# The first stage of a chunked-attention and mixture-of-experts kernel in another order, and its score products in 64x64 tiles of TensorE

## The chip, the cores and the metric

The kernel runs on one core of a Trainium2 chip, in one launch. The metric is device time in microseconds (us) of one execution. The engines are TensorE (PE in the profile, with PEld for its weight loads), VectorE (DVE), ScalarE (ACT), GpSimd (POOL) and SyncE (SP), which here only issues transfers. The kernel before takes 537.81 us (median of 3 runs, 537.52 to 538.01).

## The reference, cut to what matters

Three stages follow each other on 4 x 768 = 3072 tokens.

```
# 1. chunked linear attention, per batch and head (8 heads, head_dim 32, state 16)
cum = cumsum(log a) in a chunk;  L = exp(cum_i - cum_j) for i >= j
y   = ((C B^T) * L) x  +  exp(cum) * (C state)
state = decay * state + (B * decay_from_j)^T x
# 2. gated MLP on [3072, 256], d_ff 1536
y = (silu(x @ w_gate) * (x @ w_val)) @ w_out
# 3. routed MLP: 8 experts, one expert for each token, 256 -> 1024 -> 256, gated by its probability
```

The inputs are float32 (the MLP's weights are float64 and come as pairs of 32-bit words). The output is float32, [3072, 256].

## The kernel before, in words

The sequence is cut into 24 units of 128 tokens of one batch, numbered u, six for each batch. Four units make a block of 512 tokens; there are six blocks. For each unit four things happen in the first of the reference's stages:

- `weigh(u)` (L274) multiplies x by the decays W, on VectorE or GpSimd, into `xw`.
- `scores_mm(u)` (L282) makes on TensorE the state products (L292, into `pc`, 64 columns) and the score products (L298, B C^T, 256 columns, same buffers). Both use tiles of the array of 64 rows and 32 columns, eight of which work side by side. Each product is one of float32 and appears in the trace as two passes, so L298 has 16 passes in a unit.
- `scores_m(u)` (L302) masks the scores on VectorE (`mt`), and `states(u)` (L309) carries the state on (`st`, `sv`, `se`).
- `values_mm(u)` (L332) makes the outputs (L344, L354, also in 64x32 tiles); `values_out(u)` and `values_low(u)` scale them on VectorE and split them into a high and a low part (`xt`, L375 and L381).

Around it, `decode(f, parts)` (L397) turns one twelfth of the MLP's weights (768 KB, loaded by `load_w`) from float64 words into a high and a low float32 part: part 0 on ScalarE, parts a, b and c on VectorE (L409, L412, L416), part 2 on ScalarE (`wh`, L419), part 3 (`wl`, L421). `mlp1_mm` (L430) and `mlp1_down` (L459) are the MLP's products, in 128x128 weights and 512 columns, three for each product of float32.

The order of all work is written out by hand: each engine executes its instructions in the order in which the program issues them, and waits come from the data and from buffers used in turn (three PSUM buffers "a" for `pc` and `py`, three "g", four for x and for C). SyncE's queue carries nearly all loads, in order.

`first_block` (L807) holds the stage that the change reorders. It loads, makes the decays of the first block (`setup_ln`, `setup_decay`, `setup_cum`), and then walks units 0 to 3: in each turn it issues the scores of unit u+1 and the values of unit u, then `keep_busy(n)`, which multiplies a constant by itself n times into a PSUM buffer that nobody reads, then the VectorE work. Decodes of the first weights stand between. After the fourth turn the MLP of block 0 begins (24 turns i, with units 4 to 11 in between), then `block(b)` for blocks 2 to 5, and at last the routed stage. `emit_d` and `emit_u` spread the decays of one block over heads (GpSimd, then TensorE and ScalarE); block 1's are wanted from unit 4 on.

Of the kernel before, what the change touches and what calls it, by code (L numbers as in the profile page):

```python
# [9 lines left out]
F32 = mybir.dt.float32  # L10
# [19 lines left out]
NBLK = T // BLK  # L30
# [90 lines left out]
def kernel(  # L121
# [5 lines left out]
    nc = tc.nc  # L127
# [34 lines left out]
    def load(u):  # L162
        if u >= NU or u in raw:
            return
        r = {}
        xbb = ap_.tile([128, 512], F32, name="xbb", tag="xbb", bufs=4)
        nc.sync.dma_start(out=xbb, in_=I["xbb"][:, u])
        r["x"] = xbb[:, 0:DM].rearrange("k (h d) -> k h d", h=8)
        r["b"] = xbb[:, DM:DM + 128]
        r["bt"] = xbb[:, DM + 128:]  # L170
        r["c"] = ap_.tile([128, 2, 4, 64], F32, name="cbd", tag="cbd", bufs=4)
        nc.sync.dma_start(out=r["c"].rearrange("p r h i -> p (r h i)"), in_=I["cbd"][:, u])
        raw[u] = r

    def setup_loads():
        nc.sync.dma_start(out=at[:, 0:2], in_=I["at"][:, 0:2])
        nc.scalar.dma_start(out=c1[:, 0:C_R16], in_=I["cst"][:, 0:C_R16])
        nc.scalar.dma_start(out=c1[:, C_R16:C1], in_=I["cst"][:, C_R16:C1])
        nc.scalar.preload_act_table_set("natural_log_exp_and_others")

    def setup_ln(b0, b1):
        a = at[:, b0:b1]
        nc.vector.tensor_scalar(out=a, in0=a, scalar1=1e-6, scalar2=1.0, op0=ALU.max, op1=ALU.min)
        nc.scalar.activation(out=a, in_=a, func=AF.Ln)

    def setup_decay(b0, b1):
        p = ps_g("pw", (128, b1 - b0, 32))
        nc.tensor.matmul(out=p, lhsT=c1[:, C_S:C_S + 128], rhs=at[:, b0:b1, 0:32], start=True, stop=True)
        nc.scalar.activation(out=W[:, b0:b1], in_=p, func=AF.Exp)
# [11 lines left out]
    def keep_busy(n):  # L201

        if not idle_t:
            idle_t.append(ps.tile([128, 2, 256], F32, tag="y0", bufs=1, name="pi"))
        for _ in range(n):
            nc.tensor.matmul(out=idle_t[0], lhsT=r32[:, 0],  # L206
                             rhs=r32.rearrange("p g j -> p (g j)").unsqueeze(1).to_broadcast([128, 2, 256]),
                             start=True, stop=True)

    def silu_first():  # L210
# [32 lines left out]
    def cum_store(b0, n, p):  # L243
        nc.vector.tensor_copy(out=eb[:, 8 * b0:8 * b0 + 8 * n], in_=p)
# [37 lines left out]
    def scores_mm(u):  # L282


        r = raw[u]
        r["pc"] = [ps_a([128, 512], "pc") for _ in range(2)]
        r["pS"] = [p[:, 256:320] for p in r["pc"]]
        for q in range(4):
            for i in range(2):
                if i == 0 or u % NC != NC - 1:  # L290
                    k = slice(64 * i, 64 * i + 64)
                    nc.tensor.matmul(out=r["pS"][i][32 * q:32 * q + 32], lhsT=r["b"][k, 32 * q:32 * q + 32],  # L292
                                     rhs=r["xw"][k, 2 * q:2 * q + 2], start=True, stop=True,
                                     tile_position=(64 * i, 32 * q))
        for q in range(4):
            for g in range(2):
                k = slice(64 * g, 64 * g + 64)
                nc.tensor.matmul(out=r["pc"][g][32 * q:32 * q + 32, 0:256], lhsT=r["bt"][k, 32 * q:32 * q + 32],  # L298
                                 rhs=r["c"][k, q // 2].rearrange("p h i -> p (h i)"), start=True, stop=True,
                                 tile_position=(64 * g, 32 * q))  # L300

    def scores_m(u):  # L302
        r = raw[u]
# [84 lines left out]
    def load_w(f, e=nc.sync):  # L388
        if f >= NF:
            return  # L390
        wr[f] = keep.tile([128, 768, 2], I32, name="wraw", tag="raw", bufs=3)
        e.dma_start(out=wr[f], in_=I["mw"][f].bitcast(I32).rearrange("p (n t) -> p n t", t=2))
# [414 lines left out]
    def first_block():  # L807

        setup_loads()
        load(0)  # L810
        nc.sync.dma_start(out=at[:, 2:], in_=I["at"][:, 2:])
        load_w(0)
        load(1)
        load(2)
        load_w(1)
        load(3)
        load_w(2)
        setup_ln(0, 2)
        setup_decay(0, 2)
        setup_cum(0, 1)  # L820
        weigh(0, nc.vector)
        scores_mm(0)
        cum_split(0, 1)
        setup_ones()
        setup_ln(2, NBLK)
        setup_decay(2, NBLK)
        scores_m(0)
        emit_u(0, emit_d(0))
        cum_store(0, 1, cum_ends(0, 1, cum_ends_d(0, 1)))
        states(0)  # L830
        cum_pairs(1, 8)
        weigh(1, nc.gpsimd)
        weigh(2, nc.gpsimd)
        keep_busy(1)
        decode(0, 0, "a", "b")
        for u in range(4):
            scores_mm(u + 1)
            values_mm(u)
            keep_busy((5, 7, 6, 7)[u])
            scores_m(u + 1)  # L840
            states(u + 1)
            values_out(u)
            if u == 0:
                decode(0, "c")
            if u == 1:
                decode(1, "a")
            if u == 2:
                decode(1, "b")
            values_low(u)
            load(u + 4)  # L850
            if u == 0:
                load_w(3)
                nc.sync.dma_start(out=c2, in_=I["cst"][:, C1:C_END])
                weigh(3, nc.gpsimd)
                decode(0, 2)
                decode(0, 3, low=nc.gpsimd)
            if u == 1:
                setup_cum(1, 2)
                decode(1, 0)
                d = emit_d(1)  # L860
                weigh(4, nc.gpsimd)
            if u == 2:
                silu_first()
                emit_u(1, d)
                weigh(5, nc.gpsimd)
        decode(1, "c", 2, 3)
        decode(2, 0)
        load_w(4)

        todo = {0: 2, 1: 3, 2: 4, 4: 5, 6: 6, 8: 7, 10: 8, 12: 9, 14: 10, 15: 11}  # L870
        units = {0: 4, 1: 5, 3: 6, 5: 7, 13: 8, 16: 9, 19: 10, 22: 11}
        for i in range(2 * NF):
            q, f = divmod(i, HALF)
            b, f = q % 2, f + HALF * (q // 2)
            u = units.get(i)
            w = todo.get(i, NF)
            if i + 1 in units and units[i + 1] > 4:
                weigh(units[i + 1] + 1, nc.vector if i < 16 else nc.gpsimd)
            if u == 7:
                scores_mm(u + 1)  # L880
                values_mm(u)
                values_out(u)
                values_low(u)
            p = mlp1_mm(b, 0, BLK, f)
            if u is not None and u != 7:
                scores_mm(u + 1)
                values_mm(u)
            if len(late) == LAG:
                mlp1_down(*late.pop(0))
            late.append((b, 0, BLK, f))  # L890
            decode(w, 1)
            h = mlp1_h(p, BLK)
            if w < NF:
                load_w(w + 3)
                decode(w + 1, 0)
            decode(w, 2)
            if u is not None and u != 7:
                values_out(u)
            decode(w, 3)
            if i in (20, 21):  # L900
                turn_y(0, 2 * i - 40)
                turn_y(0, 2 * i - 39)
            if i == 23:
                route_b(0)
            mlp1_split(h, b, 0, BLK, f)
            if i in (7, 13):
                take_part(0 if i == 7 else 1)
            if i == 19:
                take_y(0)
            if u is not None:  # L910
                if u != 7:
                    values_low(u)
                    scores_m(u + 1)
                    states(u + 1)
                load(u + 4)
            if i == 6:
                scores_m(8)
                cum_split(1, 2)
            if i == 7:
                dd.append(cum_ends_d(1, 2))  # L920
            if i == 8:
                cum_store(1, 2, cum_ends(1, 2, dd.pop()))
                cum_pairs(8, NU)
                states(8)
            if i == 9:
                dd.append(emit_d(2))
            if i == 10:
                emit_u(2, dd.pop())
            if 16 <= i < 20:
                setup_route(i - 16)  # L930
            if i == 22:
                route_a(0)
            if i == 21:
                dd.append(emit_d(3))
            if i == 23:
                emit_u(3, dd.pop())
# [190 lines left out]
```

## Time and profile before

| | before |
|---|---|
| time, median of 3 runs | 537.81 us (537.52 to 538.01) |
| time of the profiled execution | 539.36 us |
| its span | 537.6 us |
| PE busy | 510.0 us (95%), 4592 matmuls |
| DVE busy | 297.2 us (55%) |
| ACT busy | 211.5 us (39%) |
| POOL busy | 105.9 us (20%) |
| mean granted clock of TensorE | 0.984 |

The span is what the trace covers; the time of the same execution is 1.8 us longer. Shares of busy time are averages over stages: the stretches that the change touches are seen in the rows below. In a timeline row the two numbers in front are the start and the time covered, "xN" is the count of instructions merged, and brackets show how long the engine sat idle before it and what ended that.

### The profile page before, as it was taken

The page shows a single profiled execution, that of the slowest core. Times are in us where ns is not written, and L with a number is a line of the kernel's source. Part 1 is how long each engine was busy: PE and PEld are TensorE (multiplying, and loading weights), DVE is VectorE, ACT ScalarE, POOL GpSimd, SP SyncE. Part 2 cuts the span into 40 slices and gives each one's busy share as a digit, 9 for nine tenths or more (in the row PEclk, how much of TensorE's full clock was granted, in tenths as well). Part 3 has the DMA queues.
Part 4 walks back from the last instruction along what each step waited for, and adds up shares of the span by engine and source line. Part 5 has one row for each costly group of instructions (what it writes and reads, how often), then busy time and mean ns, then how long its engine had stood idle before and what let it go on. Part 6 is the DMA issues. An engine that isn't in the chain of part 4 may idle for free.

```text
span 537.6 us, 11261 instructions
## 1 busy us (share of the span) xinstructions
PE 510.0 (95%) x4592; PEld 420.9 (78%) x4592; DVE 297.2 (55%) x643; ACT 211.5 (39%) x391; POOL 105.9 (20%) x127
## 2 busy tenths in 40 slices
PE   5889899999999999999999999999999999999990
PEld 3667688778878878887778778888889989999880
DVE  5788787785454454446443555365376664646320
ACT  3454356443333333333333333344454354535220
POOL 2300000131040050003200033403036425250210
PEclk9899899999999999999999999999999999999996
DMA  8755232111023122103100102434097534431100
GB/s 291 291 178 195 101 103 93 41 51 40 22 77 28 56 63 40 40 21 100 21 2 2 41 2 62 176 104 53 2 138 165 173 118 137 143 116 41 39 21 21
DMA packets 20838, 45.84 MB, mean 85 GB/s; under 512 B 4656, under 2 KB 8496, under 8 KB 20784
## 3 DMA queue, kind: packets, MB, share of 16 engines
q1 hardware_dynamic: 17424, 38.39, 24.9%
q0 software_dynamic: 3072, 6.41, 3.8%
q8 instruction: 37, 0.61, 0.6%
q10 hardware_dynamic: 288, 0.30, 0.2%
q14 instruction: 17, 0.14, 0.1%
HBM read 38.59 MB, written 6.50 MB: 84 GB/s over the span
## 4 chain that ended last, share of the span: by engine, by line
PE 80%; issue 9%; DVE 5%; POOL 2%; DMA 1%; ACT 1%; SPq 0%; POOLq 0%; DVEq 0%
PE py L469 19%; PE pg L441 18%; PE pv L441 17%; PE ph L758 8%; PE po L779 8%; PE pt L553 2%; PE pc L298 2%; POOL out L793 1%; PE py L354 1%; PE py L344 1%; PE pi L206 1%; PE pc L292 1%; PE px L747 1%; DMA xbb<-in_xbb 1%; DVE wv L412 1%
## 5 line engine op out<-in xcount | busy, mean ns | idle before, releaser
L441 PE MATMUL pg<-xt,wh 128*128 128x512 f32 x288 | 93.6, 406 | 1.9 <-ACT wh L419 1.8
L441 PE MATMUL pv<-xt,wh 128*128 128x512 f32 x288 | 91.0, 397 | 0.6 <-DVE h L449 0.6
L449 DVE TENSOR_TENSOR h<-h,pv 128x512 f32<-128x512 f32 x72 | 49.4, 686 | 66.5 <-PE pv L441 58.0
L456 DVE TENSOR_TENSOR hl<-h,hh 128x512 fp32r<-128x512 f32 x72 | 50.3, 698 | 61.7 <-ACT hh L455 61.4
L758 PE MATMUL ph<-xt,hl 128*128 128x512 f32 x288 | 72.7, 394 | 0.0
L779 PE MATMUL po<-hl,hh 128*128 128x256 f32 x384 | 70.1, 283 | 0.0
L441 PEld LDWEIGHTS pv<-xt,wh 128*128 128x128 f32 x288 | 54.4, 190 | 14.1 <-DVE h L449 1.4
L441 PEld LDWEIGHTS pg<-xt,wh 128*128 128x128 f32 x288 | 52.5, 190 | 13.2 <-ACT wh L419 2.0
L779 PEld LDWEIGHTS po<-hl,hh 128*128 128x128 f32 x384 | 60.3, 188 | 2.1
L455 ACT CAST hh<-h 128x512 fp32r<-128x512 f32 x72 | 44.6, 620 | 41.2 <-DVE h L449 41.2
L448 ACT ACTIVATE h<-pg 128x512 f32<-128x512 f32 x72 | 42.7, 593 | 42.1 <-PE pg L441 42.1
L614 POOL DMA_INDIRECT slots<-ids,si x24 | 26.0, 1083 | 168.3 <-DVE si L606 163.5
L758 PEld LDWEIGHTS ph<-xt,hl 128*128 128x128 f32 x288 | 51.7, 188 | 9.2
L469 PE MATMUL py<-hh,wh 128*128 128x512 f32 x144 | 58.6, 407 | 0.0
L441 PE MATMUL pg<-xt,wl 128*128 128x512 f32 x144 | 57.5, 399 | 0.2 <-DVE wl L421 0.2
L441 PE MATMUL pv<-xt,wl 128*128 128x512 f32 x144 | 56.9, 395 | 0.0
L469 PE MATMUL py<-hl,wh 128*128 128x512 f32 x144 | 56.8, 395 | 0.0
L469 PE MATMUL py<-hh,wl 128*128 128x512 f32 x144 | 56.8, 395 | 0.0
L779 PE MATMUL po<-hl,hl 128*128 128x256 f32 x192 | 53.9, 281 | 0.2 <-DVE hl L767 0.2
L767 DVE SCALAR_TENSOR_TENSOR hl<-ph,hh 128x512 fp32r<-128x512 f32 x48 | 33.0, 688 | 32.9 <-ACT hh L766 32.8
L766 ACT ACTIVATE hh<-ph 128x512 fp32r<-128x512 f32 x48 | 28.8, 600 | 42.9 <-PE ph L758 27.6
L779 PEld LDWEIGHTS po<-hl,hl 128*128 128x128 f32 x192 | 36.1, 188 | 0.4 <-DVE hl L767 0.4
(140 smaller groups left out, 675.1 us busy)
## 6 DMA issues: line engine op xcount, KB each, us to landing
eraw<-in_ew SPq DMA_DIRECT2D x24, 512.0 KB, 3.8
wraw<-in_mw SPq DMA_DIRECT2D x12, 768.0 KB, 4.3
xbb<-in_xbb SPq DMA_DIRECT2D x24, 256.0 KB, 4.5
cbd<-in_cbd SPq DMA_DIRECT2D x24, 256.0 KB, 4.4
yd<-yr SPq DMA_DIRECT2D x6, 528.0 KB, 3.2
slots<-ids,si POOLq DMA_INDIRECT x24, 8.1
xg<-yd,idx POOLq DMA_INDIRECT x24, 4.9
out<-ob,idx POOLq DMA_INDIRECT x24, 2.5
```

What stands on the lines that cost most here:

```text
L298: nc.tensor.matmul(out=r["pc"][g][32 * q:32 * q + 32, 0:256], lhsT=r["bt"][k, 32 * q:32 * q + 32], rhs=r["c"][k, q // 2].rearrange("p h i ...
L441: nc.tensor.matmul(out=t, lhsT=w[:, f, o:o + 128], rhs=xt[:, xp, k, cs], start=n == 0, stop=n == 5)
L448: nc.scalar.activation(out=h, in_=p[0], func=AF.Silu)
L449: nc.vector.tensor_tensor(out=h, in0=h, in1=p[1], op=ALU.mult)
L455: nc.scalar.copy(out=hh, in_=h)
L456: e.tensor_tensor(out=hl, in0=h, in1=hh.bitcast(F32), op=ALU.subtract)
L469: nc.tensor.matmul(out=yb[b][d][:, c:c + m], lhsT=w[:, f, o:o + 128], rhs=h, start=first and n == 0, stop=last and n == 2, skip_group_chec ...
L614: i = nc.gpsimd.indirect_dma_start(out=slots[0:E * upto], out_offset=bass.IndirectOffsetOnAxis(ap=si[:, s:s + 1], axis=0), in_=ids[g][:, o ...
L758: nc.tensor.matmul(out=p, lhsT=self.hl[:, w, o:o + 128], rhs=self.xt[:, xp, k], start=n == 0, stop=n == 5)
L766: nc.scalar.activation(out=hh, in_=p, func=AF.Relu)
L767: nc.vector.scalar_tensor_tensor(out=hl, in0=p, scalar=0.0, in1=hh.bitcast(F32), op0=ALU.max, op1=ALU.subtract)
L779: nc.tensor.matmul(out=self.po[s // 2][:, s % 2], lhsT=h[:, q], rhs=self.hl[:, w, o:o + DM], start=f == 0 and n == 0 and s % 2 == 0, stop= ...
```

## The change

- `setup_loads`: the load of the table of ScalarE's functions is issued ahead of the second constants' transfer rather than behind it.
- SyncE's order: unit 1's x and C come right behind unit 0's, ahead of the other blocks' `at` and the first weights; the third weights (`load_w(2)`) come behind unit 4's loads rather than before the loop.
- The logarithms and decays of blocks 1 to 5 (`setup_ln(2, NBLK)`, `setup_decay(2, NBLK)`) and the cumulated decays for blocks 2 to 5 (`setup_cum(1, 2)`) are issued later or, for the last, one turn earlier: in the first turn of the loop. `emit_d(1)` and `emit_u(1)` move up from turns 1 and 2 to before the loop and turn 0.
- `weigh(1)` is issued on GpSimd ahead of the states of unit 0.
- Weight 0's parts a, b, c are decoded together in turn 0 (before: a and b ahead of the loop, c in turn 0).
- Constant products: 0, 2, 2 and 1 in turns 0 to 3 in place of 5, 7, 6 and 7, none ahead of the loop in place of 1, and each on float32 rather than float32r operands.
- The scores of unit 4 are issued behind the values of unit 3, and their mask and state behind `values_low(3)`.
- In all 24 units the score products use tiles of 64x64: four products (eight passes) of 256 columns in place of eight (16 passes).

```diff
     def setup_loads():
         nc.sync.dma_start(out=at[:, 0:2], in_=I["at"][:, 0:2])
         nc.scalar.dma_start(out=c1[:, 0:C_R16], in_=I["cst"][:, 0:C_R16])
+        nc.scalar.preload_act_table_set("natural_log_exp_and_others")
         nc.scalar.dma_start(out=c1[:, C_R16:C1], in_=I["cst"][:, C_R16:C1])
-        nc.scalar.preload_act_table_set("natural_log_exp_and_others")
...
-            nc.tensor.matmul(out=idle_t[0], lhsT=r32[:, 0],
-                             rhs=r32.rearrange("p g j -> p (g j)").unsqueeze(1).to_broadcast([128, 2, 256]),
+            nc.tensor.matmul(out=idle_t[0], lhsT=r32[:, 0].bitcast(F32),
+                             rhs=r32.bitcast(F32).rearrange("p g j -> p (g j)").unsqueeze(1).to_broadcast([128, 2, 256]),
                              start=True, stop=True)
...
-        for q in range(4):
+        for i in range(2):
             for g in range(2):
                 k = slice(64 * g, 64 * g + 64)
-                nc.tensor.matmul(out=r["pc"][g][32 * q:32 * q + 32, 0:256], lhsT=r["bt"][k, 32 * q:32 * q + 32],
-                                 rhs=r["c"][k, q // 2].rearrange("p h i -> p (h i)"), start=True, stop=True,
-                                 tile_position=(64 * g, 32 * q))
+                h = slice(64 * i, 64 * i + 64)
+                nc.tensor.matmul(out=r["pc"][g][h, 0:256], lhsT=r["bt"][k, h],
+                                 rhs=r["c"][k, i].rearrange("p h i -> p (h i)"), start=True, stop=True,
+                                 tile_position=(64 * g, 64 * i))
...
         load(0)
+        load(1)
         nc.sync.dma_start(out=at[:, 2:], in_=I["at"][:, 2:])
         load_w(0)
-        load(1)
         load(2)
         load_w(1)
         load(3)
-        load_w(2)
...
         setup_ones()
-        setup_ln(2, NBLK)
-        setup_decay(2, NBLK)
         scores_m(0)
         emit_u(0, emit_d(0))
+        weigh(1, nc.gpsimd)
         cum_store(0, 1, cum_ends(0, 1, cum_ends_d(0, 1)))
         states(0)
         cum_pairs(1, 8)
-        weigh(1, nc.gpsimd)
+        setup_ln(2, NBLK)
+        decode(0, 0)
+        d = emit_d(1)
         weigh(2, nc.gpsimd)
-        keep_busy(1)
-        decode(0, 0, "a", "b")
         for u in range(4):
-            scores_mm(u + 1)
-            values_mm(u)
-            keep_busy((5, 7, 6, 7)[u])
-            scores_m(u + 1)
-            states(u + 1)
+            if u < 3:
+                scores_mm(u + 1)
+                values_mm(u)
+            else:
+                values_mm(u)
+                scores_mm(u + 1)
+            if u < 3:
+                scores_m(u + 1)
+                states(u + 1)
             values_out(u)
             if u == 0:
-                decode(0, "c")
+                emit_u(1, d)
+                setup_decay(2, NBLK)
+                setup_cum(1, 2)
+                decode(0, 1)
...
+            keep_busy((0, 2, 2, 1)[u])
             values_low(u)
             load(u + 4)
             if u == 0:
+                load_w(2)
                 load_w(3)
...
             if u == 1:
-                setup_cum(1, 2)
                 decode(1, 0)
-                d = emit_d(1)
...
             if u == 2:
                 silu_first()
-                emit_u(1, d)
                 weigh(5, nc.gpsimd)
+        scores_m(4)
+        states(4)
```

## Rows read from the trace of the kernel before

**Rows 1.** Stretches: length, busy us (instructions) of each engine, granted clock, DMA share, GB/s.
```profile
12.00:18.60 6.60, 4.47 (x137) 3.33 (x134) 5.70 (x19) 2.19 (x5) 4.12 (x5) 0.99 1.04 408
18.60:22.00 3.40, 3.40 (x48) 2.46 (x54) 1.41 (x3) 1.42 (x3) 0.66 (x2) 0.51 0.93 346
30.00:60.00 30.00, 24.90 (x436) 18.38 (x434) 27.32 (x56) 15.36 (x27) 0.00 (x0) 0.99 0.49 167
60.00:63.00 3.00, 3.00 (x8) 2.38 (x9) 1.65 (x6) 1.00 (x2) 0.00 (x0) 0.52 0.92 360
80.00:310.00 230.00, 230.00 (x2321) 184.63 (x2321) 123.83 (x297) 84.84 (x174) 30.11 (x43) 1.00 0.17 44
```

**Rows 2.** Timeline of VectorE in the first stage.
```profile
10.52 0.55 DVE L409 TENSOR_SCALAR wv<-wraw 128x768 int32<-128x768 int32 x1
...
12.09 0.74 DVE L306 TENSOR_TENSOR mt<-pc,c 128x256 f32<-128x256 f32 x2
...
17.63 0.36 DVE L370 TENSOR_TENSOR y<-py,U 128x192 f32<-128x192 f32 x1 [0.83 <-PE py L354]
...
18.70 0.97 DVE L409 TENSOR_SCALAR wv<-wraw 128x768 int32<-128x768 int32 x1
...
22.25 0.76 DVE L306 TENSOR_TENSOR mt<-pc,c 128x256 f32<-128x256 f32 x2 [2.24 <-PE pc L298]
...
28.57 0.95 DVE L416 SCALAR_TENSOR_TENSOR wv<-wraw,wv 128x768 int32<-128x768 int32 x1
```

**Rows 3.** Timeline of TensorE in the first stage.
```profile
10.54 0.49 PE L292 MATMUL pc<-xw,xbb 64*32 64x64 f32 x10 [0.21 <-DVE se L317]
...
17.29 0.31 PE L354 MATMUL py<-cbd,st 64*32 64x64 f32 x5 [2.13 <-issue]
17.53 2.54 PE L206 MATMUL pi<-r 128*128 128x512 f32 x7
19.87 1.08 PE L195 MATMUL pe<-c,at 128*128 128x132 f32 x4
20.88 0.47 PE L292 MATMUL pc<-xw,xbb 64*32 64x64 f32 x16
```

**Rows 4.** Timelines of GpSimd and of ScalarE in the first stage.
```profile
9.87 0.62 POOL L279 TENSOR_TENSOR xw<-xbb,W 128x256 f32<-128x256 f32 x1 [2.48 <-DMA xbb<-in_xbb]
...
17.59 1.04 POOL L260 TENSOR_TENSOR du<-er,c 128x512 fp32r<-128x512 f32 x1
...
1.65 1.28 ACT L179 ACT_TABLE_LOAD   x1 [1.65 <-PEq L1117]
```

**Rows 5.** Timeline of TensorE around the scores and values of one unit, in the MLP.
```profile
156.62 0.40 PE L441 MATMUL pv<-xt,wl 128*128 128x512 f32 x1
156.94 0.34 PE L292 MATMUL pc<-xw,xbb 64*32 64x64 f32 x16
157.08 0.64 PE L298 MATMUL pc<-cbd,xbb 64*32 64x256 f32 x16
157.51 0.53 PE L344 MATMUL py<-mt,xw 64*32 64x64 f32 x28
157.82 0.24 PE L354 MATMUL py<-cbd,st 64*32 64x64 f32 x1
157.83 0.22 PE L344 MATMUL py<-mt,xw 64*32 64x64 f32 x1
...
157.89 0.34 PE L354 MATMUL py<-cbd,st 64*32 64x64 f32 x12
158.16 0.50 PE L469 MATMUL py<-hh,wh 128*128 128x512 f32 x1
158.50 0.40 PE L469 MATMUL py<-hh,wl 128*128 128x512 f32 x1
158.73 0.40 PE L469 MATMUL py<-hl,wh 128*128 128x512 f32 x1
```

**Rows 6.** Instructions of line 298 from 62 us on: durations in ns, first and last start.
```profile
L298 PE MATMUL pc<-cbd,xbb x240: 376/376/400, 98.0 to 305.5; 64*32 64x256 f32 x120
```

## The prediction

> **What bounds the kernel now.** I read the stretches first. From 80 to 310 us TensorE is busy in 230.00 of 230 us [rows 1]: whatever is added to its queue there is added to the end, one for one. From 30 to 60 us VectorE is busy in 27.32 of 30 us and TensorE in 24.90 [rows 1]: here the decodes on VectorE set the pace, and a stage before it that ends sooner moves this one as a whole. So I look at the first stage (to about 29 us) by where VectorE sits idle or is slowed, and at the rest by what TensorE gets more or less of.
>
> VectorE's timeline in the first stage shows two idle times that end by TensorE: 0.83 us before the `y` of unit 1 at 17.63, and 2.24 us before the mask of unit 3 at 22.25 [rows 2]. TensorE's own timeline says why. In the middle of unit 1's values it stands 2.13 us released by "issue", that is by nothing the profile shows; no instruction there waits for data, and I read it as instructions that came late [rows 3]. Then come seven constant products and four passes of `setup_cum`, 17.53 to 20.88, ahead of the scores of unit 3 that VectorE waits for [rows 3]; and 18.60 to 22.00 has a granted clock of 0.51, so all this ran at the lower of the two levels (1.2 rather than 2.4 GHz) [rows 1]. That follows on the idle 2.13 us.
>
> The last view is one unit in the MLP's part: 156.94 to 158.16 is scores, states and values, between products of 512 columns [rows 5].
>
> **The change part by part.**
>
> *Loads and start.* Unit 1's x lands just before 9.87, where GpSimd waits for it [rows 4]. Ahead of it and with it the queues carry 2022 KB (decays 64, constants 70 and 224, unit 0 512, other decays 128, weights 768, x 256); after the change 1126 KB. At the 408 GB/s of [rows 1] the 896 KB are 2.2 us: it lands near 7.7 and `xw` is there near 8.3 rather than 10.49. The other holds of the scores of unit 1 then decide: the products of `emit_u(0)` no longer stand behind the decays of the other blocks, and wait for GpSimd's `du` alone; and the scores write a buffer that unit 0's state must have been read from (before: 10.54, released by `se`, [rows 3]). The chain to that state begins with x of unit 0; 224 KB of constants now go out 1.3 us later, behind the table load (1.28 us, [rows 4]), and 224 KB at 408 GB/s are half a microsecond sooner for that x. I put the state at 8.8 rather than 10.5, the scores 8.8 to 10.2 and the mask at 10.2 rather than 12.09 [rows 2]. But parts a and b of weight 0, which ran from 10.52 until that mask, 1.57 us, now come after it. Net gain 12.09 - 10.2 - 1.57 = 0.3 us, bounds -0.7 (constants later than VectorE wants them) and +0.8. The table load itself starts sooner than at 1.65, so no logarithm waits longer for it.
>
> *Third weights later.* Issued ahead of the loop before, they now stand in SyncE's queue behind unit 4's loads, which wait until the values of unit 0 have read C. 768 KB at 408 GB/s are 1.9 us, so they land before 20 us. Their first reader, `decode(2, 0)` on ScalarE, stands behind part c of weight 1, at 28.57 [rows 2] and near 25 after: 0, under some 5 us of cover; without it the decode would be late by what is missing.
>
> *The fetch wait.* Fewer constant products and eight passes with their loads fewer in each unit's scores put the same count of TensorE instructions later, into the scores of unit 3, and the transfers that compete (share 1.04 of the engines, [rows 1]) end no later. I take the 0.83 us as gone; bounds: gone, or back as 0.8 at unit 3.
>
> *Constant products and setup_cum.* A pass of 256 columns on float32 costs 0.22 us: 16 of them on eight tiles take 157.51 - 157.08 = 0.43 us, two rounds [rows 5]. A float32 product of 512 columns is then two passes of 0.43 us, 0.86 us; two are 1.7 us, where seven took 19.87 - 17.53 = 2.34 and `setup_cum` 1.01 at the lower clock [rows 3]. `setup_cum` and the decays now stand in turn 0, beside VectorE's three decode parts of weight 0 (0.55 for a, about 0.95 for b and c each, as the rows of L409 and L416 in [rows 2]), which cover them. Unit 3's scores then come 1.7 + 0.6 us behind the values of unit 1, while VectorE works on the mask (0.76), on `y` (17.63 to 18.70, 1.1), on part a (0.55, [rows 2]) and on state and low part, together about 2.8 us by my estimate: the 2.24 us go. If the cover fails, that is if the clock falls as before, two products take 3.4 us and some 1.5 us come back. Below nothing this can't go.
>
> *`emit_d(1)` on GpSimd.* It ran at 17.59 to 18.63, and part a at 18.70 took 0.97 us where the same at 10.52 took 0.55 [rows 2, 4]. Now it runs near 8, where VectorE has little: gain 0.4, bounds 0 and 0.7.
>
> *Order of unit 4's scores and mask.* The same instructions, behind `values_low(3)`; VectorE does them ahead of part c at 28.57 [rows 2] in either order: 0.
>
> Sum for the first stage, as VectorE reaches part c of weight 1: 0.3 + 0.83 + 2.24 + 0.4 = 3.8 us sooner, bounds 2.0 and 5.0. VectorE-bound work carries this to 60 us. There 60 to 63 us has the lower clock [rows 1]; I leave these 1.5 us in.
>
> *Tiles of 64x64.* The columns that stream stay the same: eight passes on four tiles are again two rounds of 0.22 us. What is new is that the shape changes twice in a unit, from 64x32 to 64x64 behind the states and back ahead of the values. The trace of before has no such change, only 128x128 to 64x32 and back. The first costs 156.94 - 156.62 = 0.32 us where the step is 0.23 (158.73 - 158.50): 0.09 us. The way back costs more: the last pass of L354 starts at 157.89 + 0.34 - 0.23 = 158.00, its stream is about 0.05, L469 starts at 158.16, so 0.1, and then the weight load of 128 columns lies open, 158.50 - 158.16 = 0.34 against 0.23, another 0.11 [rows 5]. So a change costs between nothing (if tiles of two shapes may overlap) and 0.20 us. I take 0.09, since the loads of 64 or 32 columns are nearer to the first. From 62 us on line 298 has 240 passes [rows 6], 16 a unit: 15 units. 15 x 2 x 0.09 = 2.7 us more; bounds 0 and 15 x 2 x 0.20 = 6.0. In the four or five units before 60 us VectorE's pace hides it. That the instructions are fewer gains nothing there, as TensorE waits for none.
>
> Sum: -3.8 + 2.7 = -1.1 us. The profiled execution takes 539.36 us (span 537.6 and 1.8 around it), after it 538.3; that execution lies 1.55 us above the median of the runs, so the median goes from 537.81 to 536.7.
>
> **The rivals.**
>
> *Changes of shape cost nothing.* Tiles work independently of each other: a pass of L354 at 157.82 starts before one of L344 that stands ahead of it in the program [rows 5]. If a 64x64 tile only waits for the 64x32 tiles under it, the 2.7 us fall away: 537.8 - 3.8 = 534.0. Against it: the only shape changes that the trace has do cost something.
>
> *Each change of shape empties the array and then loads its weights in the open, as the way back to 128x128 does.* Place: the 15 units from 62 us on; price 0.20 us a change, 0.40 a unit, 6.0 in all; it decides from 3.8 / 15 = 0.25 us a unit. 537.8 - 3.8 + 6.0 = 540.0, slower. For it: the two parts of 0.1 us are in the rows [rows 5]. Against it: loads of 32 columns may be too short to show. The Trainium skill ("TensorEngine Tiling (Array Packing)", Key Properties) says that changing the tiling mode, and not just the tile, drains TensorE, and lists 64x64 and 64x32 as two configurations. By that rule it is this rival rather than the first; the trace agrees for 128x128 to 64x32 (0.32 against 0.23), and no run here shows 64x32 to 64x64.
>
> *The first stage gives little.* With 5 constant products in place of 26 TensorE has gaps, the clock falls in two turns rather than one, and the fetch wait returns at unit 3: 3.8 - 0.8 - 1.5 = 1.5 us of gain, 537.8 - 1.5 + 2.7 = 539.0. For it: the fall at 18.6 followed on a gap of 2.13 us. Against it: the two float32 products are 1.7 us of work in one piece, close to the seven (1.6 us at the full clock) they replace.
>
> **How the numbers follow.** Forecast case 0.42, no cost of shapes 0.24, full cost 0.22, little from the first stage 0.12. A measurement can tell about 0.2%, 1.1 us, from no change. The forecast case, 535.5 to 538.2 by itself, is over 0.2% faster in half of its chance; the second always; the third is slower in two thirds of its and the same in the rest; the fourth is slower in half and the same in most of the rest. Faster 0.48, same 0.29, slower 0.23. The range reaches to the second case and below it by what the first stage's bound leaves, 533.4, and up to the third, 539.9.
>
> **What would show it.** In the stage: the wait of GpSimd for unit 1's x near 7 to 8 us; no "issue" gap of 2 us in unit 1; VectorE's idle time before the mask of unit 3 under 0.5 us; part c of weight 1 near 25 us; TensorE's MLP beginning near 24 us rather than 28. In a later unit: from the first L292 to the first L344, 0.57 us now, 0.75 if I am right, 0.57 for the first rival, 0.9 or more for the second. The prediction is wrong if the 15 units add over 0.3 us each, or if VectorE stands idle for over 1.5 us in the first stage between 12 and 25 us.

## The result: slower, 542.1 us against 537.7

After the change the median is 542.10 us (four runs, 541.96 to 542.18); before, in the same comparison, 537.66 us (four runs, 537.28 to 538.01). The ratio is 1.0078, with an interval of 1.0064 to 1.0093: slower by 4.4 us, where 1.1 us faster was forecast, and outside the range.

**Profile after.** The profiled execution took 542.15 us (span 540.4), the one before 539.36 (span 537.6). The page's line on the engines: busy us, share of the span, instructions.

```profile
PE 513.7 (95%) x4384; PEld 414.4 (77%) x4384; DVE 296.9 (55%) x643; ACT 211.1 (39%) x391; POOL 105.3 (19%) x127
```

TensorE before was busy for 510.0 us in 4592 instructions: now it has fewer instructions and is busy for 3.7 us more. The stretches of the kernel after, columns as in [rows 1]:

```profile
12.00:18.60 6.60, 6.36 (x124) 3.31 (x123) 6.42 (x18) 3.62 (x9) 3.09 (x3) 1.00 0.97 351
18.60:22.00 3.40, 3.40 (x114) 1.77 (x110) 3.37 (x11) 2.05 (x5) 0.77 (x2) 1.00 1.01 379
30.00:60.00 30.00, 25.51 (x355) 18.19 (x350) 27.37 (x59) 13.99 (x27) 0.00 (x0) 0.94 0.50 181
60.00:63.00 3.00, 3.00 (x14) 2.43 (x13) 1.75 (x4) 1.19 (x3) 0.00 (x0) 1.00 0.40 153
80.00:310.00 230.00, 228.84 (x2175) 178.77 (x2174) 120.54 (x284) 82.20 (x169) 29.85 (x42) 1.00 0.16 42
```

Three things differ from [rows 1]. VectorE is now busy in 6.42 and 3.37 us of the first two stretches (5.70 and 1.41 before): its idle times there are gone. The clock is 1.00 at 18.6 to 22 and at 60 to 63, where it was 0.51 and 0.52. And TensorE, busy in all of the 230 us before, now idles 1.16 of them.

VectorE in the first stage, after (line numbers from 296 on are one higher than in [rows 2]):

```profile
10.93 0.75 DVE L307 TENSOR_TENSOR mt<-pc,c 128x256 f32<-128x256 f32 x2 [1.25 <-PE pc L299]
...
14.41 1.25 DVE L417 SCALAR_TENSOR_TENSOR wv<-wraw,wv 128x768 int32<-128x768 int32 x1
...
18.50 0.97 DVE L410 TENSOR_SCALAR wv<-wraw 128x768 int32<-128x768 int32 x1
...
19.72 0.74 DVE L307 TENSOR_TENSOR mt<-pc,c 128x256 f32<-128x256 f32 x2
...
24.10 0.36 DVE L371 TENSOR_TENSOR y<-py,U 128x192 f32<-128x192 f32 x1 [0.72 <-PE py L355]
...
26.97 0.95 DVE L417 SCALAR_TENSOR_TENSOR wv<-wraw,wv 128x768 int32<-128x768 int32 x1
```

The mask of unit 3 comes at 19.72 without a wait (22.25 before), but part c of weight 1 at 26.97 (28.57 before): 1.6 us sooner, not 3.8. TensorE and GpSimd in the same stage show what took its place:

```profile
9.28 0.46 PE L292 MATMUL pc<-xw,xbb 64*32 64x64 f32 x14 [0.35 <-DVE st L317]
9.67 1.13 PE L299 MATMUL pc<-cbd,xbb 64*64 64x256 f32 x8
...
14.74 0.66 PE L299 MATMUL pc<-cbd,xbb 64*64 64x256 f32 x8
...
23.68 0.34 PE L355 MATMUL py<-cbd,st 64*32 64x64 f32 x15 [1.36 <-issue]
...
25.48 0.96 PE L442 MATMUL pg<-xt,wh 128*128 128x512 f32 x2
```

```profile
7.24 0.61 POOL L279 TENSOR_TENSOR xw<-xbb,W 128x256 f32<-128x256 f32 x1
...
16.61 1.81 POOL L422 TENSOR_TENSOR wl<-wv,wh 128x768 fp32r<-128x768 f32 x1 [1.76 <-ACT wh L420]
18.38 0.66 POOL L279 TENSOR_TENSOR xw<-xbb,W 128x256 f32<-128x256 f32 x1
```

The wait released by nothing that the profile shows has moved from unit 1 [rows 3] to unit 3, and part a of weight 1 takes 0.97 us beside GpSimd's `xw`, as long as before [rows 2].

The unit that answers to [rows 5], TensorE after:

```profile
154.69 0.40 PE L442 MATMUL pv<-xt,wl 128*128 128x512 f32 x1
155.02 0.34 PE L292 MATMUL pc<-xw,xbb 64*32 64x64 f32 x16
155.29 0.66 PE L299 MATMUL pc<-cbd,xbb 64*64 64x256 f32 x8
155.88 0.45 PE L345 MATMUL py<-mt,xw 64*32 64x64 f32 x32
156.15 0.46 PE L355 MATMUL py<-cbd,st 64*32 64x64 f32 x16
156.54 0.50 PE L470 MATMUL py<-hh,wh 128*128 128x512 f32 x1
156.87 0.39 PE L470 MATMUL py<-hh,wl 128*128 128x512 f32 x1
```

The weight loads of the scores and of the values in that unit, after, and the passes of the scores from 62 us on, as in [rows 6]:

```profile
155.29 0.21 PEld L299 LDWEIGHTS pc<-cbd,xbb 64*64 64x64 f32 x8
155.88 0.29 PEld L345 LDWEIGHTS py<-mt,xw 64*32 64x32 f32 x32 [0.38 <-issue]
L299 PE MATMUL pc<-cbd,xbb x120: 376/402/427, 95.2 to 307.7; 64*64 64x256 f32 x120
```

and the same loads before:

```profile
157.03 0.21 PEld L298 LDWEIGHTS pc<-cbd,xbb 64*32 64x32 f32 x16
157.30 0.62 PEld L344 LDWEIGHTS py<-mt,xw 64*32 64x32 f32 x31
```

States to scores is 0.27 us (0.14 before), scores to values 0.59 (0.43); from the first value to L470 0.66 (0.65), and the open weight load of L470 is as before (0.33 against 0.34). Before, the weights of the scores begin to load 0.05 us ahead of their first product (157.03, 157.08) and those of the values 0.21 ahead (157.30, 157.51 [rows 5]); after, each load begins together with the first product (155.29, 155.88). The passes of the first of the two rounds of scores now take 427 ns; those of the second take 376, as before. Over the 15 late units, first state to first 512-column product is 1.62 to 1.66 us in 12 of after, against 1.39 or 1.40 in 13 of before; the two short ones of each (1.52 and 1.22) are this one and one near 246. So a unit costs 0.25 us more. The remaining unit of after, at 260.18, took 3.10 us: it holds the wait that the last stretch misses, shown with e7.

**Where the 4.1 us lie.** I set the change's trace beside that of e6 below, an execution of the kernel before that lay at the median (538.01 us). Its span is 536.22 us, that of the change 540.35. Part c of weight 1 starts at 26.97 us (26.90 in e6), and the last unit before the late ones at 54.24 (53.97): up to there the change gains nothing on e6. The first late unit starts at 94.88 (96.43). In between, e6 has the lower clock at 60 to 63 us and this execution of the change has not, and that stretch is 1.8 shorter. The first late unit and the next 13 cost 14 x 0.25 = 3.5 more, the late wait 1.45 more: the last late unit starts at 307.18 (303.76). That unit and the rest add another 0.7, 0.25 of it the unit itself. 0.3 - 1.8 + 3.5 + 1.45 + 0.7 is 4.1, within rounding.

### The profile page after: what moved, and what is told of

The parts are those of the page before. It is cut to its first block, busy times and chain, and to the rows that moved or that the text cites. A ratio compares the mean times of both kernels' runs of the same rounds, so it can differ in the third digit from the quotient of the medians.

```text
span 540.4 us, 10847 instructions
## 1 busy us (share of the span) xinstructions
PE 513.7 (95%) x4384; PEld 414.4 (77%) x4384; DVE 296.9 (55%) x643; ACT 211.1 (39%) x391; POOL 105.3 (19%) x127
## 4 chain that ended last, share of the span: by engine, by line
PE 76%; issue 11%; DVE 5%; POOL 2%; ACT 2%; DMA 1%; SPq 0%; POOLq 0%; DVEq 0%; ACTq 0%
PE py L470 18%; PE pg L442 17%; PE pv L442 17%; PE ph L759 6%; PE po L780 6%; PE pc L299 2%; PE pt L554 2%; POOL out L794 2%; PE py L355 1%; PE py L345 1%; PE pc L292 1%; DVE wv L413 1%; PE pi L206 1%; PE px L748 1%; POOL xg L718 1%
## 5 line engine op out<-in xcount | busy, mean ns | idle before, releaser
L470 PE MATMUL py<-hh,wh 128*128 128x512 f32 x144 | 58.6, 407 | 0.0
L470 PE MATMUL py<-hh,wl 128*128 128x512 f32 x144 | 56.9, 395 | 0.0
L470 PE MATMUL py<-hl,wh 128*128 128x512 f32 x144 | 56.8, 395 | 0.0
```

What stands on the lines that cost most here:

```text
L470: nc.tensor.matmul(out=yb[b][d][:, c:c + m], lhsT=w[:, f, o:o + 128], rhs=h, start=first and n == 0, stop=last and n == 2, skip_group_chec ...
```

## The experiments

Two theories at first: the changes of tile shape in the late units make the loss; or the reordered first stage does, and the waits that it moves. Later runs ask how far one profiled execution speaks for its kernel, and what the late wait hangs on.

**e1: the change with its scores back in 64x32 tiles.**

```
-        for i in range(2):
+        for q in range(4):
             for g in range(2):        # the score products of before
```

> The changed kernel with its score products back in 64x32 tiles; the new first stage is kept. Theory A (each change of tile shape costs TensorE, 0.256 us a unit in the changed kernel's trace, on the 15 units after 62 us): 3.8 us less than 542.1, so 538.3 us, and 536.9 us if the 1.4 us wait without a releaser near 262 us goes with it. Theory B (the loss comes from the new first stage and what its fewer instructions do later, the tile shape only moves time about): it stays at 541 to 542 us. From the first state product to the first value product of a late unit: 0.57 us by A and B alike, since only the sum is in dispute.

537.75 us against 538.05, ratio 0.9999 (0.9987 to 1.0011). Without the wide tiles the loss is gone; and the whole of the reordered stage, forecast at -3.8 us, moves the time by nothing that can be measured.

**e2: the kernel before with its scores in 64x64 tiles, nothing else.**

```
-        for q in range(4):
+        for i in range(2):            # with the products of the change
```

> The kernel before with only the 64x64 score tiles; the old first stage is kept. Theory A: 3.8 us more than 537.7, so 541.5 us, up to 543 us if a fetch wait comes as well. Theory B: 537.7 us plus at most 1 us.

542.07 us against 538.05, ratio 1.0083 (1.0069 to 1.0098). The tiles alone make the whole loss. Its late units take 1.65 us, as after, and it has no wait in any of them: of the 4.0 us between the medians (4.5 by the ratio) 0.25 x 15 = 3.8 are in the units.

**e3: the change with the scores ahead of the states,** so that a unit changes from 128x128 to 64x64 to 64x32 and has one change between the small shapes rather than two.

```
 def scores_mm(u):
+    (score products, 64x64)
     (state products, 64x32)
-    (score products, 64x64)
```

> The changed kernel with the score products issued ahead of the state products in each unit, so that the shape goes 128x128, 64x64, 64x32, 128x128: one change fewer in a unit, the same products. If the price is one of each change (theory A, 0.13 us each): 15 x 0.13 = 2.0 us less, 540.1 us. If instead 64x64 products as such are slower than 64x32 ones (theory C): no difference, 542.1 us.

543.13 us, ratio 1.0108 (1.0091 to 1.0125): the time went the other way than expected. TensorE around one unit of it (here line 292 is the scores and 299 the states):

```profile
156.78 0.40 PE L442 MATMUL pv<-xt,wl 128*128 128x512 f32 x1
157.11 0.66 PE L292 MATMUL pc<-cbd,xbb 64*64 64x256 f32 x8
157.70 0.34 PE L299 MATMUL pc<-xw,xbb 64*32 64x64 f32 x16
...
158.49 0.50 PE L470 MATMUL py<-hh,wh 128*128 128x512 f32 x1
```

The unit itself did as the shape theory says: 158.49 - 157.11 = 1.38 us against 1.52, one change fewer, and 1.56 against 1.65 in most others. So a change from 64x32 into 64x64 is worth some 0.1 us net. The other 0.16 of the 0.25 stay: scores to states take 0.59 us here, as scores to values did, and the first round of scores 427 ns. That is the change out of 64x64 and the slower first round together; e3 doesn't part the two. That the second round takes 376 ns, as before, speaks against theory C. But its late units begin at 97.45 us rather than 94.88 (e7 below, without any edit, at 97.39), and the late wait is 1.80 us in place of 1.16. The gain of 1.4 us in the units is lost to these two, which the edit was not meant to touch.

**e4: e1 without any of the constant products.**

```
-            keep_busy((0, 2, 2, 1)[u])
+            keep_busy((0, 0, 0, 0)[u])
```

> The changed kernel with 64x32 score tiles and no constant products at all in the loop. If they only keep the clock up (theory A): the granted clock falls in the first 30 us and the MLP begins no earlier, 538 to 540 us against the run with 64x32 tiles and five constant products. If they are only in the way (rival): 1 to 2 us faster than that run.

538.38 us (536.79 to 543.01), ratio 1.002 (1.000 to 1.004). The clock falls, as theory A has it (0.57 from 22 to 30 us, 1.00 in e1), but the MLP begins at 25.00 rather than 25.40 us. The profiled execution reaches the late units sooner than e1's (94.37 against 94.86) and takes 1.9 us longer from the last of them to the end. The median is no better and the runs scatter more: five products of constants are worth somewhere between nothing and two microseconds.

**e5 and e6: the kernel before, twice more.** No edit.

> The kernel before, unchanged, looked at again. Theory A (the 2.13 us wait without a releaser in unit 1 and the lower clock behind it belong to that one profiled execution, not to the kernel): no such wait or a shorter one; the mask of unit 3 near 20.6 us rather than 22.25 and the masks inside the MLP near 36.2, 42.9 and 52.6 us, as in the run with the old first stage and 64x64 tiles. Theory B (the old first stage always loses those 3 us, and the new one loses something else): 22.3, 37.6, 44.3 and 53.9 us as in the first profile.

> The same once more, to see how often the wait comes: by theory A at most one of these two looks shows it; by B both.

539.16 and 538.01 us. Waits of TensorE by what released them, total, times and longest, first e5, then e6:

```profile
PE py L354 <- issue: 1.9, 1, 1.9
```

```profile
PE py L354 <- issue: 0.8, 1, 0.8
```

VectorE's mask of unit 3 and part c of weight 1 in e6:

```profile
20.44 0.76 DVE L306 TENSOR_TENSOR mt<-pc,c 128x256 f32<-128x256 f32 x2 [0.55 <-PE pc L298]
...
26.90 0.95 DVE L416 SCALAR_TENSOR_TENSOR wv<-wraw,wv 128x768 int32<-128x768 int32 x1
```

and the stretches from 18.6 and from 60 in e6:

```profile
18.60:22.00 3.40, 3.40 (x107) 2.84 (x106) 2.81 (x9) 2.22 (x5) 0.67 (x1) 1.00 0.95 351
60.00:63.00 3.00, 3.00 (x10) 2.33 (x9) 1.11 (x2) 0.52 (x2) 0.00 (x0) 0.58 0.45 156
```

The wait of unit 1 is 2.13, 1.9, 0.8 and, in e2, whose first stage has the old order, absent. Behind the two long ones the clock of 18.6 to 22 is 0.51; where it is short or absent it is 1.00, and in e6 the 2.24 us before the mask of unit 3 are 0.55. Neither theory holds whole: both executions have the wait, as B says, but its length goes with the execution, and so does the mask of unit 3 (21.52 and 20.44). In e6 the slow passes come earlier: five constant products from 12.47 take 2.44 us there, against 1.43 in the execution that I predicted from. That one had the longest wait of the four.

**e7: the change once more.** No edit.

> The changed kernel, unchanged, looked at again: the waits without a releaser of 1.36 us (unit 3) and 1.44 us (near 262 us) stay if they hang on the place of the instructions in the program, and move or go if they hang on the execution. The 0.26 us a unit for the shapes stay in either case.

544.89 us, one run. It has no wait in unit 3 of the first stage, but ran that stage at the lower clock for longer (the score passes at 16.75 still took 1.13 us), and starts its late units at 97.39 us, not 94.88. Its late wait stands at the very place of the first execution, behind the eighteenth of the 32 passes of one unit's last products:

```profile
263.82 0.47 PE L355 MATMUL py<-cbd,st 64*32 64x64 f32 x18
265.57 0.40 PE L355 MATMUL py<-cbd,st 64*32 64x64 f32 x14 [1.27 <-issue]
```

In the first execution of the change:

```profile
261.32 0.47 PE L355 MATMUL py<-cbd,st 64*32 64x64 f32 x18
262.95 0.40 PE L355 MATMUL py<-cbd,st 64*32 64x64 f32 x14 [1.16 <-issue]
```

**e8: the change with 13 short constant products in place of 5 long ones** (196 columns rather than 512, so the same columns in all, and 32 TensorE instructions more ahead of everything later).

```
-             rhs=(constants, 512 columns)
+             rhs=(constants, 196 columns)
-            keep_busy((0, 2, 2, 1)[u])
+            keep_busy((0, 5, 5, 3)[u])
```

> The changed kernel with its five constant products of 512 columns cut into 13 of 196 (0, 5, 5 and 3 in the turns): the same work of TensorE within 0.1 us, but 32 instructions more, which brings the count of TensorE's instructions to that of the run with the old first stage and 64x64 tiles, where no wait stood near 262 us. Theory A (that wait, 1.4 to 2.0 us in three looks, comes from where the program's instructions fall, and TensorE waits for them): it goes, 540.7 us. Theory B (it comes from what the first stage left behind in transfers or buffers): it stays, 542.1 us. The 0.26 us a unit for the shapes stay in both.

541.71 us, ratio 1.0058 (1.0035 to 1.0080). The wait goes, as theory A has it, but the time is nearer to the 542.1 of B than to 540.7, and the interval overlaps that of the change (1.0064 to 1.0093). Its profiled execution starts the late units at 96.77 us, 1.9 later than the change's first. The same unit of it:

```profile
263.20 0.59 PE L355 MATMUL py<-cbd,st 64*32 64x64 f32 x32
263.73 0.50 PE L470 MATMUL py<-hh,wh 128*128 128x512 f32 x1
```

**e9: the same split with the narrow tiles,** that is the reordered stage without its tiles of 64x64.

> The same 13 constant products with the score products in 64x32 tiles: the count of TensorE's instructions of the kernel before, with the new first stage. Theory A: the wait of 0.8 us near 198 us that the run with 64x32 tiles and five constant products showed goes; 1.5 us less where the clock does not fall near 60 us; 536.9 us, against 538.0 before. Theory B: as the run with five constant products, 537.8 us.

536.98 us (536.09 to 538.08) against 538.01, ratio 0.9976 (0.9960 to 0.9992): the fastest of all, a little ahead of the kernel before and some 5 us ahead of the change. It comes at the 536.9 of theory A in part by luck: the 1.5 us of the clock, which are in that sum, its profiled execution did not gain (the clock is 0.50 from 58 to 60 us). e1 had a short late wait of its own, which e9 has not. TensorE in e1:

```profile
200.29 0.33 PE L354 MATMUL py<-cbd,st 64*32 64x64 f32 x6 [0.52 <-issue]
```

**The ratios side by side:**

| first stage | tiles 64x32 | tiles 64x64 |
|---|---|---|
| old | 1 | 1.0083 |
| new | 0.9999 | 1.0078 |
| new, products split | 0.9976 | 1.0058 |

Along each row the tiles cost 0.8%, 4.3 to 4.5 us (4.0 to 4.7 between the medians). Down each column the new stage gives nothing. With the constant products split it gives 0.2% with the narrow tiles; with the wide ones the intervals of 1.0058 and 1.0078 overlap, and a gain isn't shown.

## Why the prediction was wrong

**"Sum for the first stage ... 3.8 us sooner, bounds 2.0 and 5.0": the failed step.** 0.83 and 2.24 of the 3.8 us were idle times of one execution. That one lay 1.55 us above its own median, as I noted, but I then took the gain off the median all the same, as if those 1.55 us would stay in both kernels. They were in good part the idle time that I was removing: in e6, at the median, the two read 0.44 (before `y` of unit 1) and 0.55. Part c of weight 1, by which I counted the gain, starts at 28.57, 27.97, 26.90 and 27.17 us with the old stage (before, e5, e6, e2) and at 26.97, 29.52, 26.89, 28.19, 26.49, 28.83 and 26.32 with the new (after, e7, e1, e3, e4, e8, e9). The means are 27.65 and 27.60: no gain, where single executions with the new stage differ by 3.2. The three earliest have the new stage and narrow tiles (e1, e4, e9), so a small gain with those is not excluded. The bounds were wrong as well: those of the parts add up to 0.0 and 4.6, not to 2.0 and 5.0, and the range never put the low end of the stage together with the high end of the tiles. Its parts:

- *Start, +0.3.* The load was right: `xw` of unit 1 ran at 7.24 us without a wait. But state and scores came at 9.28 rather than 8.8, the scores took 1.13 us at the lower clock, and the mask came at 10.93, not 10.2. With 1.57 us of weight parts moved behind it that is a loss of 0.4.
- *The fetch wait, 0.83.* Its other bound came true: 1.36 us at unit 3, and behind it 0.72 us of VectorE's idle time. My reading of it, instructions that come late, has support in its place. Wherever a trace has this wait in the first stage, it stands ahead of the same passes, counted from TensorE's first: the 219th (before 2.13, e5 1.90, e6 0.81, e9 0.12 us) or the 345th (after 1.36, e3 0.32, e4 1.59, e9 1.25). Yet e4 has no constant products and e9 has 13, so other work stands there. What delays it, and why its length goes with the execution, is not shown.
- *The 2.24 us before the mask of unit 3.* Gone, as forecast, with the clock of 18.6 to 22 at the upper level in this execution; in e7 the mask waited 2.08 us. I had put all of 17.53 to 20.88 at the lower level, but the clock up to 18.60 is 0.99 [rows 1], so the first microsecond of it was not.
- *GpSimd beside VectorE, 0.4.* Not gained: part a of weight 1 took 0.97 us again, and part c of weight 0 took 1.25 where I had 0.95, beside an `xw` that began at 13.75. I had misread the row: `du` had ended at 18.63, before part a began at 18.70. What ran beside part a was `xw` (18.59 to 19.25), and the change doesn't move that out of its way.

**"I leave these 1.5 us in."** This is the term that moved. From the last unit before the late ones to the first late one it takes 42.2 to 42.5 us in the executions with the lower clock between 57 and 63 us (before, e5, e6, e2, e3, e9) and 40.6 to 40.9 in those without (after, e7, e1, e4, e8). So both executions of the change gained some 1.6 us here, which I had put at nothing. But e3 and e9, with the new stage, have the lower clock too, and what decides it is not shown. The late units therefore start at 97.85, 97.49, 96.43 and 96.67 us with the old stage (before, e5, e6, e2) and at 94.88 and 97.39 in the change (after, e7).

**"15 x 2 x 0.09 = 2.7 us more": right in kind, too small.** The units cost 0.25 us each, 3.8 in all, that is 0.13 a change. I had taken for both the 0.09 of the row that enters a smaller shape, and left out the weight load that lies open on the way back to 128x128. The rows of the loads above show it open at both changes. The column count was right, the scores stayed at two rounds, but the first of them takes 0.05 us longer.

**The rivals.** *Changes cost nothing* is refuted by e2. *Each change empties the array and loads in the open* was right in sign and in its point of decision: 0.25 us a unit is that point, and the result was slower. Its mechanism is what the rows show, with weight loads that no longer run ahead of the first product of the scores and of the values; its size, 0.40 a unit, was too large. The rule of the Trainium skill ("TensorEngine Tiling (Array Packing)", Key Properties) that a change of tiling mode drains TensorE agrees with the rows of the unit, where states to scores take 0.27 us rather than 0.14, also for two shapes that differ in their columns alone. *The first stage gives little* was right in kind and still too high: the fetch wait did come back at unit 3, the clock of 18.6 to 22 did not fall in the first execution of the change, and of its 1.5 us nothing is seen at part c. What happened is these last two together, which no case of mine held: 537.8 + 3.8 = 541.6.

**Not in any case:** the late wait, 1.45 us with what surrounds it, 0.5 us behind the last unit, and against them the 1.8 us of the clock's stretch. With the 0.3 us by which the unit at 54 us comes later, 541.6 becomes 542.1. e8 and e9 show that it goes with 32 more instructions ahead of it; but e4, with 20 fewer than e1, has its wait (0.55 us) behind the same pass as e1 (0.52), so a plain count of instructions doesn't place it. What TensorE waits for there stays open; so does whether the 0.2% of e9 is this wait alone.

**The signs named beforehand.** First state to first value product: 0.86 us (0.75 forecast, 0.9 for the drain). MLP at 25.48, not near 24; part c of weight 1 at 26.97, not near 25. VectorE idle between 12 and 25 us: 0.72, under the 1.5 named, so the stage's local signs came out nearly as forecast while its worth did not.

## What to carry to other kernels

Idle time read in one execution is worth what it is at the median: look at two or three executions before a wait is taken off the time, and where the profiled one lies above the median, ask whether the wait is the reason. Compare the same instruction in several executions of both kernels, as part c here, before a later gain is put down to an earlier stage. A change of tile shape inside a TensorE-bound loop has a price (some 0.13 us net here), so half the instructions at the same columns can be the slower form; count the changes first. An edit that alters the instructions ahead can put a wait hundreds of microseconds later, so test the parts of a change each by itself.

## What the hardware showed unexpectedly

- TensorE stood 1.16 to 1.80 us at one place in late units, released by nothing that the profile shows, in two of two executions of the change and in e3; never there in the kernel before (three executions).
- The wait of the first stage goes by the count of TensorE's passes and not by the work that stands there: ahead of the 219th or the 345th in seven executions of five programs, 0.12 to 2.13 us long, and absent in four others.
- Behind a change between 64x32 and 64x64 the weights began to load only together with the first product of the new shape (155.29 and 155.88 us), where the same loads ran 0.05 and 0.21 us ahead without a change of shape.
- In the first stage the granted clock can't be read from the stretches: they show 1.00 at 9.67 us, where eight score passes took 1.13 us, against 0.66 for the same passes at 14.74. Durations tell the level there.
- Order alone made one unit 0.09 us shorter (e3, 1.56 against 1.65), with the same instructions.
